# Scores two steps further ahead, later reciprocals and an even projection pace in a four-layer attention and Fourier kernel

## The chip, the cores and the metric

The program runs on one core of one Trainium2 chip. The metric is the time of one execution on the device in microseconds (us). A core has engines that run side by side, each with its own queue of instructions: TensorE (PE in the profile; its weight loads are listed as PEld), VectorE (DVE), ScalarE (ACT), GpSimd (POOL), and SyncE (SP), whose queue issues nearly all DMA transfers of this kernel. An instruction waits in its queue until the semaphores it names have been raised by other engines, and everything behind it waits with it. Matmuls write into eight banks of an accumulator memory (the tile `banks` in the profile), from which ScalarE or VectorE copy results away.

## The reference

Four layers on x of 2048 rows and 640 columns: attention, Fourier mixing, attention, Fourier mixing, each on the layernorm of x and added back. The change lies in attention, which has 32 heads of width 20, each row looking at itself and the 255 rows before it.

```python
qkv = (x @ wqkv).reshape(B, S, 3, H, Dh)          # q, k, v of (H, S, Dh)
scores = jnp.einsum("bhqd,bhkd->bhqk", q, k) * (Dh ** -0.5)
mask = (idx[:, None] - idx[None, :] >= 0) & (idx[:, None] - idx[None, :] < W)   # W = 256
p = _softmax(jnp.where(mask[None, None], scores, -1e9))
o = jnp.einsum("bhqk,bhkd->bhqd", p, v)
return o.reshape(B, S, D) @ wo
# Fourier layer: Cr @ (x @ Dr) - Ci @ (x @ Di), with cosine and sine matrices
```

All matmuls of the projections are done in three products of split numbers (a high part and a rest), for precision.

## The kernel before

An attention layer is `before_heads`, `heads` (L606) and `after_heads`. Before the heads, layernormed x is transposed into four row blocks of 512 (tiles `big0` to `big3`), v is computed, and so are the first two of ten chunks of the query and key projection. A chunk is 128 columns of the joined weights (tile `wc`) for all four row blocks. The other eight chunks are computed inside `heads`.

`heads` handles 32 heads as 8 quads of 4 heads, and 2048 rows as 16 blocks of 128, so there are 128 pairs of quad and block. The loop at L777 runs over steps from -LEAD to 128. In each step three things at different places of the 128 pairs are issued:

- *scores and maxima* at s = step + LEAD: L631 multiplies queries by keys for the four heads (two pairs, z = 0 and z = 1), and L636 on VectorE adds the mask and takes each row's maximum. Every fourth step (s divisible by 4) L644 transposes the maxima of four blocks on TensorE, L647 copies them, and L649 sends them by DMA as extra rows into the query tile `qp`.
- *exponentials* at t = step: L659 multiplies the other way round (keys by queries, with the row of maxima), L669 takes the exponential on ScalarE, and L675 and L679 blank the corners on GpSimd.
- *values* at v = step - 1: L694 multiplies probabilities by values, L701 copies the result to the tile `ou`, and every fourth step `finish` (L705) posts the load of the row sums (`sm`, L711), the store of the results (`o_d`, L712), the reciprocals (L714, VectorE) and their store (`r_d`, L717). The three numbers in `at` (L710) are the ticks at which these go out; a step has two ticks.

Steps below 0 have scores only; they are called the lead here. The banks of scores, exponentials and values are handed out by a planner's clock (`borrow`), from banks 0 to 3 in the lead and 0 to 5 after.

The projection fills what room TensorE has. It is cut into units of two matmuls of 64 x 512 on two halves of the array (`lockstep`, L257). Two row blocks make a set of two banks: 15 units on one half of the rows of the weights, then 15 on the other. Between the halves the second half waits for a small VectorE copy, `seen` (L263). A chunk is two sets, 60 units; the eight chunks have 480. When a set is done its two banks are copied by ScalarE (L544), cast and subtracted on GpSimd (L552, L211), and stored to `qk_d` (L524). From there `pack` (L582) posts twelve DMAs for each quarter of a quad (L594, three a step over four steps), into `qp` and `kp` of the next quad. They are due eight steps ahead of the scores that need them (six for quad 7), by the list `due` (L726). `fill(nf)` (L752) issues about nf units, rounded so that a half is divided evenly, after z = 0 of every step, and after z = 1 too in the lead. In the lead FIRST = 7 gives 8 and 7 units a step, 15 in all, and afterwards RATE = 4 gives four, four, four and three.

A set takes its two banks from a role (L48). Role `m` has banks 6 and 7 only; role `f` has 6, 7, 4 and 5, so that in the lead two sets are open at once, their halves one after the other.

```python
ROLES = {
    "m": (6, 7), "f": (6, 7, 4, 5), "w": (6, 7, 2, 3),
```

When the projection is done, the same `fill` issues partial output rows (`partials`, nine units a step, L257 with 64 x 320 and an addition L978) from the finished quads. They need o and its reciprocals loaded again from DRAM (`load_o`, L859 and L865) and x (L952). These start at step 97 in this kernel.

Of the kernel before, what the change touches and what calls it, by code (L numbers as in the profile page):

```python
# [21 lines left out]
NQ = H // 4  # L22
# [4 lines left out]
SCALE = DH ** -0.5  # L27
EPS = 1e-5

LEAD = 10  # L30
AHEAD = 8
EARLY = 3
AHEAD_X = 4
AFTER = 4
RATE = 4
FIRST = 7
LATE = 9
BACK = 2
PACE = 0.65
# [25 lines left out]
class Net:  # L65
# [89 lines left out]
    def next(self, name):  # L155
        i = self.turn.get(name, 0)
        self.turn[name] = i + 1
        tiles = getattr(self, name)[:3]
        return tiles[i % len(tiles)]
# [407 lines left out]

    def project(self):
        for c in range(2, NCH):
            lead = self.lead  # L570
            for sbs in ((0, 1, 2, 3),) if lead else ((0, 1), (2, 3)):
                if sbs[0] == 0 and c > 2:
                    self.load_chunk(c + 1)
                if sbs[-1] == 3:
                    self.cut_chunk(c + 1)
                if c == NCH - 1:
                    self.prepare(sbs[0])
                yield from self.pieces(c, sbs, "f" if lead else "m")
        self.prepare(4)
# [26 lines left out]
    def heads(self, xsrc, xdst, hook):  # L606
# [7 lines left out]
        def defer(d, fn):  # L614
            later.setdefault(now[0] + d, []).append(fn)
# [3 lines left out]
        def load_v(n):  # L619
            if n < 4 * NQ:  # L620
                nc.sync.dma_start(self.vq[n % 3][:, :384].rearrange("p (t c) -> p t c", c=96),
                                  self.vd[n // 4][:, n % 4 * 4:n % 4 * 4 + 4, :])
# [82 lines left out]
        def finish(quad, bk):  # L705
            ou = ous.pop((quad, bk))
            sm = pool.tile([P, 16], F32, name="sm", tag="sm")
            rc = pool.tile([P, 16], F32, name="rc", tag="rc")
            cols = slice(bk * 512, (bk + 1) * 512)
            at = (2, 9, 11) if quad < NQ - 1 else (1, 5, 6)  # L710
            self.post(at[0], lambda: nc.sync.dma_start(sm, ou[0:P:32, :]))  # L711
            self.post(at[0], lambda: nc.sync.dma_start(  # L712
                self.od[4 * quad:4 * quad + 4, :, cols].rearrange("h r s -> (h r) s"), ou))
            self.post(at[1], lambda: nc.vector.reciprocal(out=rc, in_=sm))  # L714

            def store():
                nc.sync.dma_start(  # L717
                    self.rd[bk, 4 * quad:4 * quad + 4, :].rearrange("h (a b) -> (h a) b", b=16), rc)
                self.post(2 if quad < NQ - 1 else 0, lambda: self.stored.add((quad, bk)))
            self.post(at[2], store)  # L720

        per_piece = 3 * KC
        total = NCH * NSB * per_piece
        done = [2 * NSB * per_piece]
# [27 lines left out]
        def fill(n):  # L752

            k, size = 0, 1
            while k < size:
                r = more()
                if r == 0 and k == 0:
                    continue
                if r != 1:
                    return  # L760
                k += 1
                if k == 1:
                    left = self.left + 1
                    size = -(-left // max(1, round(left / n)))
            if self.left == 0:
                more()
                if self.lead:
                    relieve()
                elif self.heavy:
                    self.heavy.sort(key=lambda h: h[0] not in ROLES["m"])  # L770
                    self.relieve()
# [4 lines left out]
        self.ring6 = dict.fromkeys((0, 1, 2, 3), -99.0)  # L776
        for step in range(-LEAD, steps + 1):  # L777
            now[0] = self.step = step
            clock = step * STEP
            if step == -1:  # L780
                self.ring6.update({4: -99.0, 5: -99.0})
            if step + LEAD == steps + 1:
                for b in ROLES["w"]:
                    self.ring6.pop(b, None)
            self.wide, self.lead, self.tiled = step + LEAD > steps, step < -2, step < steps - 1
            for f in later.pop(step, []):
                f()
            s, t, v = step + LEAD, step, step - 1
            if due and s >= due[0][0]:
                while done[0] < due[0][1]:  # L790
                    fill(15)
                q, j = due.pop(0)[2:]
                for i, f in enumerate(self.pack(q, j)):
                    defer(i // 3, f)
                for f in later.pop(step, []):
                    f()
            if v >= 0 and v % 4 == 3:
                load_v(v // 4 + 2)
            if done[0] < total:
                nf = max([FIRST if t < -2 else RATE + (t < 0)]  # L800
                         + [(d - done[0]) / max(1, at - s) for at, d, _, _ in due])
            else:
                nf = LATE
            rows = ((s - 1) // 16, ((s - 1) % 16) // 4) if 4 <= s < steps + 4 and s % 4 == 0 else None
            for z in range(2):
                if 0 <= t < steps:
                    banks = self.borrow_pair(clock + AT_T[z], HELD_T)
                    t_pair(t // 16, t % 16, z, banks)
                if 0 <= s < steps:
                    for e, b in enumerate(self.borrow(clock + AT_S[z], *HELD_S)):  # L810
                        s_head(s // 16, s % 16, 2 * z + e, b)
                if z and (rows or 0 <= v < steps):
                    last, = self.borrow(clock + AT_PV, HELD_PV)
                m = m_rows(*rows, last) if z and rows else iter(())
                next(m, None)
                if 0 <= t < steps:
                    t_exp(t // 16, t % 16, z, banks)
                    t_mask(t // 16, t % 16, z)
                if self.heavy:
                    self.heavy.sort(key=lambda h: h[0] not in ROLES["m"])  # L820
                    self.relieve()
                if z:
                    if 0 <= v < steps:
                        pv(v // 16, v % 16, last)
                    for _ in m:
                        pass
                if z == 0 or t < -1 or t >= steps:
                    fill(nf)
                self.tick()
            if step >= steps:  # L830
                self.load_to(step - steps + 2)
            if step > 16 * (NQ - 1):
                self.poll_late(step - 16 * (NQ - 1))
# [5 lines left out]
    def load_o(self, o, sb, k, raw=None, rr=None):  # L839
# [46 lines left out]

        busy = self.step + LEAD < 16 * NQ
        n, lane, eng = (2, "pool", nc.gpsimd) if busy else (1, "dve", nc.vector)
# [977 lines left out]
```

## Time and profile before

| what | us |
|---|---|
| median of the runs (lowest, highest) | 2182.82 (2181.66, 2192.8) |
| the profiled execution, its own time | 2187.93 |
| its span from the first to the last instruction | 2186.2 |
| heads of the first attention layer, lead to the last value | 404.1 |
| heads of the second attention layer | 401.2 |
| lead steps -10 to -3, first and second layer | 31.20, 30.70 |
| steps 0 to 91, first and second layer | 252.1, 252.2 |
| steps 97 to 117, first and second layer | 73.4, 72.9 |

The stages were cut where the first instruction of a step starts on TensorE: the first L631 for steps of the lead, the first L659 from step 0 on. A window's row has its length and then, for each engine, the microseconds in which it was busy and in brackets the number of its instructions; PE and PEld are the matmuls and the weight loads of TensorE. A row of the timeline has the start, the time taken by the whole group, the engine, the line of the kernel, and how many alike instructions were joined (x8); in brackets stands how long the engine was idle ahead of it and who ended that. A row of the kind "L544 ACT ACTIVATE x64: 578/599/609" gives minimum, median and maximum in nanoseconds. A row of waits names the engine and line that waited, who ended it, the sum, how often, and the longest. The granted clock is 1.00 nearly all through; it was half for 6.8 us in the first layer's heads (422.3 us) and for 3.4 us each at 599.8 and 1685.2.

### The profile page before, as it was taken

The page shows a single profiled execution, that of the slowest core. Times are in us where ns is not written, and L with a number is a line of the kernel's source. Part 1 is how long each engine was busy: PE and PEld are TensorE (multiplying, and loading weights), DVE is VectorE, ACT ScalarE, POOL GpSimd, SP SyncE. Part 2 cuts the span into 40 slices and gives each one's busy share as a digit, 9 for nine tenths or more (in the row PEclk, how much of TensorE's full clock was granted, in tenths as well). Part 3 has the DMA queues.
Part 4 walks back from the last instruction along what each step waited for, and adds up shares of the span by engine and source line. Part 5 has one row for each costly group of instructions (what it writes and reads, how often), then busy time and mean ns, then how long its engine had stood idle before and what let it go on. Part 6 is the DMA issues. An engine that isn't in the chain of part 4 may idle for free.

```text
span 2186.2 us, 48927 instructions
## 1 busy us (share of the span) xinstructions
PE 2118.1 (97%) x17872; PEld 1783.2 (82%) x17872; DVE 1603.7 (73%) x3931; ACT 1140.5 (52%) x2125; POOL 958.0 (44%) x1562
## 2 busy tenths in 40 slices
PE   7999999988999999999999999999899999999999
PEld 7987777677878888889999877776778888888899
DVE  6358888886897868786661588888767968677676
ACT  3117777656554545452341177777565645445332
POOL 3037776765614222322430377767655033231324
PEclk9999999999999999999999999999999999999999
DMA  5546666785555354656645556567855454546653
GB/s 183 175 157 190 198 180 215 211 224 169 202 192 189 127 183 141 214 177 207 207 156 167 162 186 200 181 212 226 216 161 182 140 182 132 174 152 208 222 165 125
DMA packets 227089, 398.40 MB, mean 182 GB/s; under 512 B 39969, under 2 KB 86561, under 8 KB 226849
## 3 DMA queue, kind: packets, MB, share of 16 engines
q1 hardware_dynamic: 226848, 395.28, 57.3%
q8 instruction: 141, 2.31, 0.5%
q14 instruction: 100, 0.81, 0.1%
HBM read 273.94 MB, written 120.06 MB: 180 GB/s over the span
## 4 chain that ended last, share of the span: by engine, by line
PE 78%; DVE 7%; DMA 5%; ACT 4%; issue 3%; POOL 2%; SPq 1%; ACTq 0%; DVEq 0%; POOLq 0%
PE banks L1416 29%; PE banks L239 15%; PE banks L257 12%; PE banks L694 6%; PE banks L659 5%; PE banks L1704 5%; PE banks L631 5%; DMA qp<-qk_d 2%; DVE banks L636 1%; ACT pt L669 1%; DMA x_d<-x 1%; PE banks L341 1%; DMA kp<-qk_d 1%; ACT big L1039 1%; DVE qp L232 1%
## 5 line engine op out<-in xcount | busy, mean ns | idle before, releaser
L636 DVE CUSTOM_DVE_ANT_0 banks<-banks,mask 128x384 f32<-128x384 f32 (+2 forms) x1024 | 527.6, 557 | 123.0 <-PE banks L631 99.9
L669 ACT ACTIVATE pt<-banks 128x768 f32<-128x768 f32 (+2 forms) x512 | 393.8, 772 | 168.7 <-PE banks L659 55.2
L675 POOL TENSOR_SCALAR_AFFINE_SELECT pt<-pt 128x256 f32<-128x256 f32 x512 | 213.3, 417 | 213.8 <-ACT pt L669 192.0
L257 PE MATMUL banks<-big,wc 64*128 64x512 f32 x1920 | 271.1, 394 | 0.4 <-DVE pt L442 0.4
L659 PE MATMUL banks<-qp,kp 61*128 61x384 f32 (+2 forms) x1024 | 210.2, 381 | 22.8 <-DVE mc L636 17.4
L694 PE MATMUL banks<-pt,vq 128*32 128x128 f32 x5760 | 211.6, 278 | 3.5 <-ACT pt L669 3.4
L631 PE MATMUL banks<-kp,qp 60*128 60x384 f32 (+2 forms) x1024 | 205.5, 347 | 6.7 <-DVE mc L636 3.1
L257 PEld LDWEIGHTS banks<-big,wc 64*128 64x128 f32 x1920 | 186.8, 185 | 22.6 <-ACT x L544 1.5
L679 POOL TENSOR_SCALAR_AFFINE_SELECT pt<-pt 128x256 f32<-128x256 f32 x448 | 193.8, 433 | 0.0
L226 ACT ACTIVATE qp<-pt 128x512 fp32r<-128x512 f32 (+1 forms) x200 | 123.2, 625 | 128.1 <-DVE pt L1347 51.7
L232 DVE TENSOR_TENSOR qp<-pt,qp 128x512 fp32r<-128x512 f32 (+1 forms) x198 | 156.6, 798 | 42.1 <-ACT qp L226 40.5
L694 PEld LDWEIGHTS banks<-pt,vq 128*32 128x32 f32 x5760 | 142.4, 110 | 51.5 <-issue 35.3
L659 PEld LDWEIGHTS banks<-qp,kp 61*128 61x128 f32 x1024 | 108.0, 184 | 87.3 <-DVE mc L636 65.2
L1416 PE MATMUL banks<-qp,big 128*128 128x512 f32 x648 | 152.9, 390 | 0.0
L631 PEld LDWEIGHTS banks<-kp,qp 60*128 60x128 f32 x1024 | 123.6, 186 | 31.9 <-DVE mc L636 16.4
L1345 POOL TENSOR_TENSOR pt<-pt,pt 128x512 f32<-128x512 f32 x32 | 47.2, 1475 | 231.4 <-DMA pt<-c 173.4
L226 ACT ACTIVATE c<-pt 128x512 fp32r<-128x512 f32 x146 | 90.4, 625 | 111.1 <-POOL pt L1325 57.1
L636 DVE DVE_READ_ACCUMULATOR2_ANT mc<- 128x1 f32 x1024 | 145.0, 142 | 0.0
L1416 PEld LDWEIGHTS banks<-qp,big 128*128 128x128 f32 x648 | 120.8, 188 | 24.2
L232 DVE TENSOR_TENSOR c<-pt,c 128x512 fp32r<-128x512 f32 x144 | 113.8, 793 | 26.9 <-ACT c L226 24.4
L1416 PE MATMUL banks<-qp,xc 128*128 128x512 f32 x480 | 117.4, 391 | 4.3 <-DVE xc L232 2.8
L552 POOL CAST c<-x 128x512 fp32r<-128x512 f32 x64 | 38.9, 611 | 166.5 <-ACT x L544 162.3
(253 smaller groups left out, 4479.9 us busy)
## 6 DMA issues: line engine op xcount, KB each, us to landing
pt<-c SPq DMA_DIRECT2D x166, 512.0 KB
qk_d<-c SPq DMA_DIRECT2D x80, 512.0 KB
kp<-qk_d SPq DMA_DIRECT2D x384, 80.0 KB
qp<-qk_d SPq DMA_DIRECT2D x384, 80.0 KB
kp<-u_d SPq DMA_DIRECT2D x32, 640.0 KB
o_d<-ou SPq DMA_DIRECT2D x64, 256.0 KB
x_d<-x SPq DMA_DIRECT2D x48, 320.0 KB
v_d<-pt SPq DMA_DIRECT2D x16, 768.0 KB
```

The source lines that it names most:

```text
L226: nc.scalar.activation(hi, src, AF.Copy, scale=-1.0 if neg else 1.0)
L232: (eng or nc.vector).tensor_tensor(out=lo, in0=src, in1=hi.bitcast(F32), op=OP.subtract)
L239: self.nc.tensor.matmul(p, x, y, start=n == 0, stop=n == last)
L257: self.nc.tensor.matmul(ps[a], x[r], y[r], start=half + i == 0, stop=half == 1 and i == n - 1, skip_group_check=True)
L631: nc.tensor.matmul(p, qp[quad % 2][b:b + 60, z, qb * P:(qb + 1) * P], kp[quad % 2][b:b + 60, z, k0 * P:(qb + 1) * P], start=True, stop=True)
L636: nc.vector.tensor_tensor_reduce(out=p, in0=p, in1=self.mask[:, 384 - n * P:], scale=1.0, scalar=NEG, op0=OP.add, op1=OP.max, accum_out=mc ...
L659: nc.tensor.matmul(self.banks[:, banks[e], :n * P], kp[quad % 2][b:b + 61, z, kb * P:(kb + 1) * P], qp[quad % 2][b:b + 61, z, kb * P:(kb + ...
L669: nc.scalar.activation(pt[quad, kb][:, 2 * z:2 * z + 2, :n * P], self.banks[:, b0:b1 + 1, :n * P], AF.Exp, scale=SCALE)
L675: nc.gpsimd.affine_select(out=t[:, :, 0:P], in_=t[:, :, 0:P], pattern=[[0, 2], [1, P]], compare_op=OP.is_ge, fill=0.0, base=0, channel_mul ...
L679: nc.gpsimd.affine_select(out=t[:, :, 256:384], in_=t[:, :, 256:384], pattern=[[0, 2], [-1, P]], compare_op=OP.is_gt, fill=0.0, base=0, ch ...
L694: nc.tensor.matmul(self.banks[32 * h:32 * h + 32, bank, :P], vq[:, 96 * (kb % 4) + 21 * h:96 * (kb % 4) + 21 * h + 32], t[:, h, (qb - kb) ...
L1416: nc.tensor.matmul(self.banks[:, bk, :], p, b[q], start=start and m == 0, stop=stop and last and m == 2, skip_group_check=True)
```

## The change

Five edits, all in `heads` and what it calls:

- LEAD is 12 instead of 10: scores and maxima run two steps further ahead, there are two more lead steps, and scores end at step 115 instead of 117.
- In the lead only chunk 2 is computed on four banks; chunk 3 and later use two banks, set after set.
- The pace after the lead is not 4 a step but the units left over the steps left until step 96. In the lead FIRST = 6 still gives 8 and 7.
- The list `due` is kept, and so is LATE.
- The reciprocals and their store go out at ticks 12 and 14 instead of 9 and 11, except for the first quarter of quad 5, which keeps the old ticks, and for quad 7, which keeps its own.

```diff
-LEAD = 10
+LEAD = 12
...
-RATE = 4
-FIRST = 7
+ROWS_AT = 96
+FIRST = 6
...
     def project(self):
         for c in range(2, NCH):
-            lead = self.lead
+            lead = self.lead and c == 2
             for sbs in ((0, 1, 2, 3),) if lead else ((0, 1), (2, 3)):
...
-            at = (2, 9, 11) if quad < NQ - 1 else (1, 5, 6)
+            at = (1, 5, 6) if quad == NQ - 1 else (2, 9, 11) if (quad, bk) == (NQ - 3, 0) else (2, 12, 14)
...
             if done[0] < total:
-                nf = max([FIRST if t < -2 else RATE + (t < 0)]
+                nf = max([FIRST if t < -2 else (total - done[0]) / max(1, ROWS_AT - t)]
                          + [(d - done[0]) / max(1, at - s) for at, d, _, _ in due])
```

The units of an attention layer come out like this in the built programs:

| steps | before | after |
|---|---|---|
| full lead steps | 8 steps, 15 units each | 10 steps, 15 units each |
| steps -2 and -1 | 10 and 5 | 8 and 4 |
| steps 0 to 91 | 345 | 306 |
| steps 92 to 95 | 0 | 12 |
| steps of three units, four units (0 to 95) | 23, 69 | 66, 30 |
| of these with a transpose of maxima | 0, 23 | 16, 8 |

*TensorE, lead, chunk 3, the end of the first half of its first set* (`big0` and `big1` are row blocks 0 and 1, `big2` and `big3` blocks 2 and 3; `wc_1190` holds the chunk's weights; in brackets the engine that is waited for). Before:

```order
L257 MATMUL banks_74<-big0_158,wc_1190 128x512
L257 MATMUL banks_74<-big1_341,wc_1190 128x512
L631 MATMUL banks_74<-kp0_561,qp0_106 128x384 [waits DVE_49] x2
L257 MATMUL banks_74<-big2_512,wc_1190 128x512 [waits Activation_49]
L257 MATMUL banks_74<-big3_732,wc_1190 128x512 [waits Activation_49]
L257 MATMUL banks_74<-big2_512,wc_1190 128x512
```

After:

```order
L257 MATMUL banks_74<-big0_158,wc_1190 128x512
L257 MATMUL banks_74<-big1_341,wc_1190 128x512
L631 MATMUL banks_74<-kp0_561,qp0_106 128x384 [waits DVE_49] x2
L257 MATMUL banks_74<-big0_158,wc_1190 128x512 [waits DVE_49]
L257 MATMUL banks_74<-big1_341,wc_1190 128x512
```

Before, the first half of the second set follows on two other banks, whose copies belong to a set that ended more than a step earlier. After, the second half of the same set follows, and it waits for the copy `seen` between the halves.

*TensorE, the end of that first set, half a step later.* After:

```order
L257 MATMUL banks_74<-big0_158,wc_1190 128x512
L257 MATMUL banks_74<-big1_341,wc_1190 128x512
L631 MATMUL banks_74<-kp0_561,qp0_106 128x384 [waits DVE_49] x2
L257 MATMUL banks_74<-big2_512,wc_1190 128x512 [waits Activation_49]
L257 MATMUL banks_74<-big3_732,wc_1190 128x512 [waits Activation_49]
```

The second set now starts on the same two banks, so its first unit waits for the ScalarE copies of the set that ended just ahead of the two L631.

*SP's queue, first layer, the first loads of quad 7* (`kp1` and `qp1` from `qk_d`) and the first o loads of the output rows (L859, L865). Before:

```order
L594 DMA kp1_104<-qk_d_82 20x2x512 x3
L952 DMA big2_5880<-x 128x640
L859 DMA x_6074<-o_d_85 128x1x512
L865 DMA rr2_103<-r_d_86 128x1x512
L859 DMA x_6077<-o_d_85 128x1x512
L711 DMA sm_6057<-ou1_100 128x1x16
L712 DMA o_d_85<-ou1_100 128x512
L717 DMA r_d_86<-rc_5906 128x16
L594 DMA qp1_105<-qk_d_82 20x2x512 x3
L859 DMA x_6147<-o_d_85 128x1x512
L865 DMA rr0_101<-r_d_86 128x1x512
```

After:

```order
L594 DMA kp1_104<-qk_d_82 20x2x512 x6
L717 DMA r_d_86<-rc_5712 128x16
L594 DMA qp1_105<-qk_d_82 20x2x512 x3
L621 DMA vq1_93<-v_d_83 128x384
L952 DMA big2_6044<-x 128x640 x2
L649 DMA qp0_106<-mt_6056 2x4x128 x2
L594 DMA qp1_105<-qk_d_82 20x2x512 x3
L952 DMA big2_6044<-x 128x640
L859 DMA x_6094<-o_d_85 128x1x512
```

Before, the o loads and the store of a quad's results stand between the loads of keys and queries; after, all twelve loads of the quarter come first.

## The prediction

> **What bounds the kernel now.** I read the page first, then a table of windows over the stages of one attention layer, then single steps, and last the rows of the instructions that the change moves.
>
> ```profile
> span 2186.2 us, 48927 instructions
> PE 2118.1 (97%) x17872; PEld 1783.2 (82%) x17872; DVE 1603.7 (73%) x3931; ACT 1140.5 (52%) x2125; POOL 958.0 (44%) x1562
> PE 78%; DVE 7%; DMA 5%; ACT 4%; issue 3%; POOL 2%; SPq 1%; ACTq 0%; DVEq 0%; POOLq 0%
> ```
>
> TensorE leads both the busy shares and the chain of waits, but these are means over stages. The windows cut the second attention layer's heads into the eight full lead steps, steps -2 and -1, steps 0 to 91, steps 92 to 96 (no projection left), steps 97 to 117, and the end without scores. Columns: length, then busy time and instructions per engine, granted clock, DMA share, GB/s.
>
> ```profile
> core 0: us, PE busy (x) PEld busy (x) DVE busy (x) ACT busy (x) POOL busy (x), PEclk, DMA share, GB/s
> 1216.90:1247.60 30.70, 30.70 (x276) 26.54 (x277) 19.65 (x73) 4.24 (x9) 11.30 (x17) 1.00 0.43 139
> 1247.60:1252.10 4.50, 4.50 (x41) 3.46 (x38) 3.37 (x12) 1.35 (x3) 3.41 (x6) 1.00 0.64 239
> 1252.10:1504.30 252.20, 247.73 (x3495) 187.72 (x3491) 210.05 (x787) 184.41 (x336) 184.44 (x422) 1.00 0.63 197
> 1504.30:1517.50 13.20, 11.58 (x165) 7.43 (x161) 11.83 (x43) 8.56 (x19) 11.21 (x24) 1.00 0.81 247
> 1517.50:1590.40 72.90, 65.23 (x1009) 53.96 (x1009) 59.56 (x201) 42.53 (x76) 44.88 (x99) 1.00 0.82 216
> 1590.40:1618.10 27.70, 25.07 (x399) 19.85 (x395) 12.29 (x23) 20.06 (x38) 20.35 (x43) 1.00 0.48 144
> ```
>
> The lead has TensorE busy all 30.70 us: there it is the bound. In steps 0 to 91 it shows 247.73 of 252.20, but its ends are modelled and its weight loads fill only 187.72, so single steps must say what a unit of projection (two matmuls) costs. Step 24 of that layer carries four units, from one first L659 to the next:
>
> ```profile
> 1318.20 0.44 PE L659 MATMUL banks<-qp,kp 61*128 61x384 f32 x2
> 1318.66 1.09 PE L257 MATMUL banks<-big,wc 64*128 64x512 f32 x8
> 1319.59 0.34 PE L659 MATMUL banks<-qp,kp 61*128 61x384 f32 x2
> 1320.85 0.44 PE L659 MATMUL banks<-qp,kp 61*128 61x384 f32 x2
> 1318.83 0.82 ACT L669 ACTIVATE pt<-banks 128x768 f32<-128x768 f32 x1 [0.21 <-PE banks L631]
> 1320.05 0.81 ACT L669 ACTIVATE pt<-banks 128x768 f32<-128x768 f32 x1 [0.41 <-DVE mc L636]
> ```
>
> It takes 2.65 us. The second exponential ends at 1320.86, where the next step's scores begin: beside TensorE there is a loop of scores, exponential and freed banks, about as long as the step. Whole steps show the price (rows: a new set's first units, three units, four units, four units with a transpose of maxima, and two with none):
>
> ```profile
> 1306.90:1309.80 2.90, 2.90 (x44) 2.12 (x40) 2.34 (x9) 2.64 (x6) 2.90 (x7) 1.00 0.44 143
> 1315.60:1318.20 2.60, 2.60 (x42) 1.93 (x38) 1.76 (x9) 2.05 (x4) 1.69 (x5) 1.00 0.76 273
> 1318.20:1320.90 2.70, 2.70 (x46) 2.15 (x42) 1.90 (x7) 1.91 (x3) 1.38 (x4) 1.00 0.60 175
> 1323.50:1326.40 2.90, 2.90 (x45) 2.35 (x41) 2.56 (x10) 1.91 (x4) 1.65 (x5) 1.00 0.62 183
> 1504.30:1506.90 2.60, 2.51 (x36) 1.60 (x32) 2.31 (x9) 2.12 (x5) 2.60 (x7) 1.00 0.64 211
> 1506.90:1509.50 2.60, 2.17 (x36) 1.46 (x33) 2.32 (x10) 1.79 (x3) 2.60 (x7) 1.00 0.62 184
> ```
>
> A step without any unit still takes 2.60, one with three takes 2.60, one with four 2.65: in the body a unit is mostly covered by the loop.
>
> **The change, per attention layer.** (1) *Two more lead steps.* Each full lead step is 30.70 / 8 = 3.84 us and holds 15 units, which stay at 15. Two more cost 7.7. The transposes of the maxima come on steps -8, -4 and 0 instead of -6 and -2, so the lead holds one more (0.28, below): **+8.0**. TensorE is wholly busy there, so nothing hides it.
>
> ```profile
> 1224.41 0.36 PE L631 MATMUL banks<-kp,qp 60*128 60x384 f32 x2
> 1224.58 2.01 PE L257 MATMUL banks<-big,wc 64*128 64x512 f32 x16
> 1226.41 0.36 PE L631 MATMUL banks<-kp,qp 60*128 60x384 f32 x2
> L257 PE MATMUL banks<-big,wc 64*128 64x512 f32 x290 | 42.4, 395 | 0.0
> L544 ACT ACTIVATE x<-banks x64: 578/599/609, 137.1 to 1504.2; 128x512 f32<-128x512 f32 x64
>   PEld banks L257: 1.5, 9
> L263 DVE COPY seen<-banks x60: 153/159/163, 129.6 to 1607.1; 128x2 f32<-128x2 f32 x60
> L644 PE MATMUL banks<-ident,mc x64: 277/277/278, 142.9 to 1592.3; 128*16 128x128 f32 x64
> ```
>
> The first three rows give a unit's price on a full TensorE: from 1224.58 to 1226.41 sixteen matmuls issue, 1.83 / 8 = 0.23 us a unit.
>
> (2) *Two banks in the lead.* Only chunk 2 now runs on four banks. From chunk 3 on, a new set's first unit waits for the two L544 copies of the set just ended, with one pair of L631 between. The last matmul's 0.39, then two copies of 0.60, less the pair's 0.36, leave 1.2 to 1.3 us of TensorE standing, at the starts of steps -6 and -4: +2.6. Likewise both halves of a set, with only that pair between, now wait for L263: 0.39 and 0.16, less the pair's 0.36, and a hand-over between engines, about 0.25 each, three times, +0.7. Sum **+3.3**. The same waits in the whole trace cost 1.5 us in nine, but in the body 1.3 us and more of other work stands between (1319.59 to 1320.85 above, and the next scores). Bounds: 0, if copies start earlier than the order says, and 5, with three full copy waits and the L631 pair hiding nothing. Behind the waiting L257 stand the next L631, so the maxima slip too; nobody waits for these yet.
> The Trainium skill, "Perfetto Trace Analysis", section "Matmuls", says that independent matmul groups should rotate through different banks, so that the evacuation of one overlaps the next group's matmuls; this speaks against the edit, and by it the +3.3 would be the result, where the nine waits of this trace alone, 0.17 each, would make it +0.5.
>
> (3) *Steps -2 and -1* hold 12 units instead of 15 (-0.7) but, by the order, a third copy wait at -2 (+1.1): **+0.4**.
>
> (4) *Steps 0 to 95.* 345 units before, 318 after, and the last 12 of these in steps 92 to 95, which had none. Of 24 transposing steps 16 have three units where all had four but one: (2.90 - 2.60) less the transpose's own share, 0.2 each, -3.2. Of the plain steps 27 more have three units: 2.65 - 2.59, so -1.5. One set fewer is started, -0.3 (2.90 against 2.65). Units in 92 to 95 hide behind POOL, which is busy 2.60 of 2.60 there, 0.05 each: +0.2. Sum **-4.8**. Bounds: 0, since a step with no unit is no shorter, and -9.0, 39 units less in steps 0 to 91 at 0.23. I take the middle, since the rows of steps lie near the low end and only the dear steps promise more.
> Of rule and row: the Trainium skill, "Perfetto Trace Analysis", section "Identifying the Most-Contended Engine", holds matmul busy time to be no good measure of how full TensorE is, and weight-load busy a better one; here that is 74% (187.72 of 252.20) against 98%. By it the price stays near the step rows; by the 98% it would be -9.0.
>
> (5) *First loads of quad 7.*
>
> ```profile
> PE banks L631 <- DMA qp<-qk_d: 2.0, 1, 2.0
> PE banks L631 <- DMA kp<-qk_d: 1.0, 1, 1.0
> PE banks L659 <- DMA qp<-mt: 1.1, 1, 1.1
> 412.90:427.80 14.90, 13.27 (x167) 8.52 (x163) 12.40 (x45) 8.70 (x19) 12.11 (x26) 0.81 0.67 213
> 1525.77 2.27 SPq L594 DMA_DIRECT2D qp<-qk_d  x3
> 1531.11 1.26 SPq L594 DMA_DIRECT2D qp<-qk_d  x3
> ```
>
> The scores of quad 7 waited 2.0 us in the second layer and 1.0 in the first, since their loads stand on SP's queue behind o loads, a reciprocal's store and the vq load. In the new order all twelve come ahead of the first o loads: **-1.5**. Bounds: -2.0, and +1.5 if now the o loads come late for the first output rows, which wait behind them. The first layer's 1.1 on a row of maxima lies in a stretch of clock 0.81; taken as gone, -1.1 once.
>
> (6) *Scores end two steps earlier.*
>
> ```profile
> 1584.00:1587.40 3.40, 3.10 (x56) 2.57 (x52) 2.98 (x10) 2.54 (x5) 1.85 (x5) 1.00 0.65 184
> 1587.40:1590.40 3.00, 3.00 (x52) 2.54 (x52) 2.79 (x12) 1.97 (x3) 2.88 (x6) 1.00 0.49 133
> 1599.50:1602.40 2.90, 2.74 (x46) 2.25 (x46) 0.75 (x2) 1.93 (x4) 2.63 (x6) 1.00 0.74 242
> L714 DVE RECIPROCAL rc<-sm x64: 240/248/254, 186.3 to 1624.0; 128x16 f32<-128x16 f32 x64
> ```
>
> Steps 116 and 117 take 3.40 and 3.0, a like step without scores 2.9: **-0.6**. *Reciprocals* move by half a step or more on VectorE, which has 42 us free in steps 0 to 91 (0.46 a step): 0. If that cover is gone, because one now stands ahead of a maximum that frees a bank, each costs its 0.25, at most 28 of them, +7. Their r_d stores move behind on SP's queue, and the first output rows, at step 97, need none of the later ones.
>
> Sum: 8.0 + 3.3 + 0.4 - 4.8 - 1.5 - 0.6 = +4.8 a layer, two layers +9.6, less 1.1: **+8.5 us**. The profiled execution took 2187.93 us, 1.7 of it outside the span; it would become 2196.4. It stood 5.1 above the median of the runs, so against the median the forecast is 2182.82 + 8.5 = **2191.3**.
>
> **The rivals.** *R1, the body gains at full price.* TensorE is the bound throughout, so moved units are free and those taken away from the body pay 0.23, while the copies hide. Per layer 8.0 - 0.7 - 9.0 - 1.5 - 0.6 = -3.8, in all -8.7: 2174. For it: 98% busy, transposing steps of 2.90 with weight loads of 2.35. Against: step 23 with two matmuls fewer is 0.06 shorter, not 0.23. If instead all 96 steps reached 2.59 (252.2 and four empty steps, 10.4, against 248.6: -14.0) the sum comes to the same, with (2) at its price.
>
> *R2, the copies are hidden.* (2) is 0 and (3) -0.7: per layer +0.4, in all -0.3: 2182.5. For it: nine copy waits cost 1.5 us. Against: just two L631 between.
>
> *R3, slower: the loop sets every body step.* If score, exponential, bank and POOL leave no step below what it has, (4) is 0, and if the loads in (5) keep their place in time, since L594 also waits for the pieces' stores, that is 0 too: per layer 8.0 + 3.3 + 0.4 - 0.6 = +11.1, in all 2205. It decides if three-unit transposing steps still take 2.8 or more. For it: the 2.60 us of empty steps; against: the 2.90 of the four-unit ones.
>
> *R4, the stores behind the later reciprocals hold up output rows.* A block of rows waits 1.5 steps, 3.9 us, once a layer: 8.5 + 7.8, 2199. Against: the one block that opens the output rows keeps its old ticks.
>
> **How the numbers follow.** Forecast 0.38, R1 0.24, R2 0.16, R3 0.16, R4 0.06. Half a per cent, 10.9 us, is about what a measurement of this kernel tells from no change. Faster (below 2171.9): somewhat over half of R1's own spread of 2165 to 2182, with a little of R2, 0.16. Slower (above 2193.7): R3, R4 and two fifths of the forecast's own spread of 2184 to 2199, 0.38. Same: 0.46. Range 2171 to 2206: R1's better third and R3's worse half, hardly 0.2 together, lie outside.
>
> **What would show it.** Ten lead steps of 3.84 with TensorE standing over 1 us, L257 waiting for L544, at steps -6, -4, -2; a body of 96 steps near 258 us where it was 262.6; transposing steps near 2.7; no wait of L631 for quad 7's loads. Wrong if lead steps stay wholly busy (R2), if the body falls below 254 (R1) or stays above 261 (R3), or if L257 of the output rows waits for loads (R4).

## The result, and the profile after

| | us |
|---|---|
| kernel before, median of 5 runs | 2188.61 |
| changed kernel, median of 5 runs (lowest, highest) | 2203.74 (2201.75, 2208.12) |
| ratio, after to before, with its 95% interval | 1.0078 [1.0062, 1.0094] |
| span of the profiled execution, before and after | 2186.2, 2199.8 |
| heads of the first layer, before and after | 404.1, 415.3 |
| heads of the second layer, before and after | 401.2, 410.4 |

The change makes the kernel slower by 0.8%, 15 us by the medians and 17 by the ratio; 8.5 was forecast. The forecast added its 8.5 to a median of three runs of the kernel before, 2182.82; with five runs it is 2188.61. The page of the changed kernel has TensorE a point higher on the chain of waits:

```profile
span 2199.8 us, 48960 instructions
PE 79%; DVE 7%; DMA 5%; ACT 3%; issue 2%; POOL 2%; SPq 1%; ACTq 0%; DVEq 0%; POOLq 0%
```

The windows over the stages of the second layer's heads, cut like those of the kernel before: ten full lead steps, steps -2 and -1, 0 to 91, 92 to 96, 97 to 117, and the end.

```profile
core 0: us, PE busy (x) PEld busy (x) DVE busy (x) ACT busy (x) POOL busy (x), PEclk, DMA share, GB/s
1222.30:1264.70 42.40, 40.85 (x343) 32.96 (x344) 23.84 (x90) 5.59 (x12) 15.89 (x24) 1.00 0.44 149
1264.70:1270.00 5.30, 4.42 (x34) 3.03 (x30) 3.67 (x12) 1.80 (x4) 4.27 (x6) 1.00 0.65 210
1270.00:1518.10 248.10, 244.05 (x3411) 181.63 (x3411) 208.62 (x785) 182.07 (x328) 174.64 (x409) 1.00 0.62 190
1518.10:1532.50 14.40, 13.72 (x190) 9.41 (x186) 12.31 (x44) 10.47 (x22) 12.08 (x25) 1.00 0.71 206
1532.50:1604.80 72.30, 64.70 (x1001) 52.98 (x1001) 55.66 (x186) 42.75 (x78) 47.09 (x103) 1.00 0.79 226
1604.80:1632.70 27.90, 24.67 (x398) 19.82 (x402) 10.68 (x21) 19.81 (x36) 20.41 (x44) 1.00 0.49 147
```

Stage by stage against before: the lead +11.7, steps -2 and -1 +0.8, steps 0 to 91 -4.1, steps 92 to 96 +1.2, steps 97 to 117 -0.6, the end +0.2: 9.2 us, the whole of 410.4 less 401.2. The loss is the lead; steps 0 to 91 give a third of it back. In the lead TensorE is no longer busy throughout (40.85 of 42.40), and the timeline of TensorE shows why. The starts of step -6 (chunk 3's second set) and of step -4 (chunk 4's first), each with the units ahead of it:

```profile
1244.07 1.75 PE L257 MATMUL banks<-big,wc 64*128 64x512 f32 x14
1245.66 0.34 PE L631 MATMUL banks<-kp,qp 60*128 60x384 f32 x2
1246.64 2.37 PE L257 MATMUL banks<-big,wc 64*128 64x512 f32 x15 [0.65 <-ACT x L544]
1253.39 1.75 PE L257 MATMUL banks<-big,wc 64*128 64x512 f32 x14
1254.98 0.34 PE L631 MATMUL banks<-kp,qp 60*128 60x384 f32 x2
1255.96 0.99 PE L257 MATMUL banks<-big,wc 64*128 64x512 f32 x3 [0.65 <-ACT x L544]
```

Behind the last unit of a set comes one pair of L631, then TensorE stands 0.65 us until the first L544 copy frees its bank; weight loads of L257 wait for copies too, so step -6 as a whole is 1.18 us longer. From first L631 to first L631, steps -7 to -3 took 4.14, 4.97, 4.35, 5.59 (with a transpose) and 4.16 us where a full lead step of the kernel before took 3.79. Over the whole trace the rows of L544, and below them those of L714, say:

```profile
L544 ACT ACTIVATE x<-banks x64: 591/597/624, 133.9 to 1528.9; 128x512 f32<-128x512 f32 x64
  PEld banks L257: 9.1, 18
  PE banks L257: 3.9, 6
L714 DVE RECIPROCAL rc<-sm x64: 195/245/254, 199.3 to 1638.5; 128x16 f32<-128x16 f32 x64
who waited for it (us, times):
```

Waits for copies grew from 1.5 us (nine times) to 9.1 at the weight loads and 3.9 at the matmuls, six of these 0.65 each: three a layer, where the prediction put them, though each is shorter than the 1 us that it named. No engine waits for the reciprocals.

The wait for quad 7 did not go. Before, queries for its first block were late at step 102; now those for its second quarter (blocks 4 to 7) are, at step 104. First the second layer's, on TensorE's timeline; then the waits and the window of that step in the first layer:

```profile
1555.70 0.41 PE L631 MATMUL banks<-kp,qp 60*128 60x384 f32 x1
1557.63 0.41 PE L631 MATMUL banks<-kp,qp 60*128 60x384 f32 x1 [1.52 <-DMA qp<-qk_d]
```

```profile
PE banks L631 <- DMA qp<-qk_d: 1.7, 1, 1.7
PE banks L631 <- DMA qp<-mt: 1.3, 1, 1.3
455.60:464.70 9.10, 6.12 (x53) 4.66 (x53) 3.83 (x11) 2.22 (x4) 3.76 (x9) 0.62 0.72 199
```

The first layer stood 1.7 and 1.3 us there, with a granted clock of 0.62 over a step of 9.1 us.

Heads grew by 20.4 us in the two layers, the span only by 13.6. The rest of these two profiles differs by 6.8 the other way: the first heads start 3.2 us earlier, and in the Fourier layers the waits of L1704 for L1540 are 2.3 us in three where they were 7.5 in six. Each view has its heading and one row of it, first of the kernel before and then of the changed kernel:

```profile
its engine sat idle before it (us, times) until:
  DVE pt L1540: 7.5, 6
```

```profile
its engine sat idle before it (us, times) until:
  DVE pt L1540: 2.3, 3
```

In the profiles of the experiments this wait lies between 2.4 and 6.3 us without following any one edit, so I count it to no part of the change; how much of it belongs to single executions stays open.

### The profile page after: what moved, and what is told of

Its sections match the earlier page's. It is cut to its first block, busy times and chain, and to the rows that moved or that the text cites. A ratio compares the mean times of both kernels' runs of the same rounds, so it can differ in the third digit from the quotient of the medians.

```text
span 2199.8 us, 48960 instructions
## 1 busy us (share of the span) xinstructions
PE 2132.3 (97%) x17872; PEld 1783.3 (81%) x17872; DVE 1593.9 (72%) x3931; ACT 1143.2 (52%) x2125; POOL 954.0 (43%) x1562
## 4 chain that ended last, share of the span: by engine, by line
PE 79%; DVE 7%; DMA 5%; ACT 3%; issue 2%; POOL 2%; SPq 1%; ACTq 0%; DVEq 0%; POOLq 0%
PE banks L1416 30%; PE banks L239 15%; PE banks L257 11%; PE banks L694 6%; PE banks L1704 6%; PE banks L659 5%; PE banks L631 5%; DVE banks L636 2%; DMA qp<-qk_d 2%; ACT pt L669 1%; DMA qk_d<-c 1%; PE banks L341 1%; ACT big L1039 1%; POOL rs L1087 1%; DVE qp L232 1%
## 5 line engine op out<-in xcount | busy, mean ns | idle before, releaser
L257 PE MATMUL banks<-big,wc 64*128 64x512 f32 x1920 | 278.1, 396 | 4.8 <-ACT x L544 3.9
L659 PE MATMUL banks<-qp,kp 61*128 61x384 f32 (+2 forms) x1024 | 207.9, 379 | 21.3 <-DVE mc L636 16.6
L631 PE MATMUL banks<-kp,qp 60*128 60x384 f32 (+2 forms) x1024 | 219.4, 358 | 6.3 <-DMA qp<-qk_d 3.4
L257 PEld LDWEIGHTS banks<-big,wc 64*128 64x128 f32 x1920 | 188.0, 185 | 30.9 <-ACT x L544 9.1
L659 PEld LDWEIGHTS banks<-qp,kp 61*128 61x128 f32 x1024 | 106.3, 184 | 86.3 <-DVE mc L636 62.4
L631 PEld LDWEIGHTS banks<-kp,qp 60*128 60x128 f32 x1024 | 126.5, 185 | 42.7 <-DVE mc L636 23.9
```

What stands on the lines that cost most here:

```text
L257: self.nc.tensor.matmul(ps[a], x[r], y[r], start=half + i == 0, stop=half == 1 and i == n - 1, skip_group_check=True)
L631: nc.tensor.matmul(p, qp[quad % 2][b:b + 60, z, qb * P:(qb + 1) * P], kp[quad % 2][b:b + 60, z, k0 * P:(qb + 1) * P], start=True, stop=True)
L659: nc.tensor.matmul(self.banks[:, banks[e], :n * P], kp[quad % 2][b:b + 61, z, kb * P:(kb + 1) * P], qp[quad % 2][b:b + 61, z, kb * P:(kb + ...
```

## The experiments

Three theories were set against each other. A: the lead pays, two steps and the bank waits. B: lead waits are made up for later. C: pace, reciprocals and SP's queue take the time. The kernel before was timed beside all eleven runs; its medians there were 2189.03 to 2189.39. To give the ratios in us I multiply by 2189.

**Four banks for chunk 3.**

```diff
-            lead = self.lead and c == 2
+            lead = self.lead and c <= 3
```

> The changed kernel, but chunk 3 too is computed on four banks in the lead. Theory A (the lead pays: two steps of 3.79 us each and 3.8 us of bank and half-boundary waits a layer): the waits at the starts of steps -7, -6 and -5 go (0.35 + 1.2 + 0.55) and part of that at -4, so 2 to 3 us a layer, 4 to 6 in all: 9 to 11 us above the kernel before instead of 15. Rival B (the waits in the lead are made up for in the body, where the copies then come later): no change, 15 above. Rival C (the time goes in the body and in SP's queue, not in the lead): no change either, with the lead shorter in the trace and the body longer.

Measured: 2200.61, ratio 1.0054 [1.004, 1.0068], 12 us above before. The window over its ten lead steps:

```profile
1221.50:1260.50 39.00, 38.92 (x345) 31.54 (x344) 24.41 (x90) 5.60 (x12) 16.47 (x24) 1.00 0.48 157
```

39.0 where the changed kernel took 42.4: 3.4 us a layer, and TensorE is busy again. The body stayed the same (steps 1 to 91: 244.7 and 245.2 against 244.8 and 244.6). The lead is as A has it, and B falls for the body. In the times the gain is 5 us (A had 4 to 6, and 9 to 11 above the kernel before), though the two intervals just overlap. Not all of its 7 by the lead is kept: in the second layer step 104 took 7.91 us here, against 6.04.

**Ten lead steps**, with the banks of before; pace and reciprocals of the change stay.

```diff
-LEAD = 12
+LEAD = 10
-            lead = self.lead and c == 2
+            lead = self.lead
```

> The changed kernel with ten lead steps and its banks as before: only the even pace and the later reciprocals are left of the change. Theory A: all of the 11.8 us a layer in the lead go and some 3 us of body come back: within 4 us of the kernel before, so 12 to 18 us below the changed kernel. Rival C (the pace and the reciprocals cost the time): 8 us or more above the kernel before.

Measured: 2183.89, ratio 0.9979 [0.9968, 0.999], 5 us below the kernel before. The whole loss of the change is in LEAD and the banks that go with it: 22 us against the changed kernel, more than A's 12 to 18. Against the run ahead it is 16 us, 8.2 a layer, which is the net of two lead steps (39.0 less 30.6, 8.4 in the traces) and of all that shifts with them. C falls. But the scores' wait got worse here; TensorE and the granted clock at step 102 of the second layer:

```profile
1526.96 0.45 PE L659 MATMUL banks<-qp,kp 61*128 61x384 f32 x2 [0.76 <-DMA qp<-mt]
1530.47 0.44 PE L631 MATMUL banks<-kp,qp 60*128 60x128 f32 x1 [2.98 <-DMA qp<-qk_d]
1530.48 2.94 PE L257 MATMUL banks<-big,big 64*128 64x320 f32 x18
```

```profile
1526.00:1528.00 2.00, 0.74 (x11) 0.40 (x3) 0.94 (x6) 1.46 (x4) 1.50 (x4) 1.00 0.92 251
1528.00:1530.50 2.50, 0.03 (x2) 0.06 (x2) 0.00 (x0) 0.32 (x1) 1.46 (x3) 0.58 0.88 216
1530.50:1533.90 3.40, 3.40 (x24) 3.14 (x24) 0.80 (x3) 0.13 (x1) 0.00 (x0) 0.50 0.77 187
```

Here TensorE stands 3 us and then works at half its clock for 3.4 us more: eighteen matmuls take 2.94, where such eighteen took 1.48 to 1.49 at the full clock.

**Old ticks of the reciprocals**, on the changed kernel.

```diff
-            at = (1, 5, 6) if quad == NQ - 1 else (2, 9, 11) if (quad, bk) == (NQ - 3, 0) else (2, 12, 14)
+            at = (2, 9, 11) if quad < NQ - 1 else (1, 5, 6)
```

> The changed kernel with the old ticks of the reciprocals and their stores. Theory A: hidden, within 3 us of the changed kernel (12 to 18 us above the kernel before). Rival C: if a reciprocal between the two halves of a step holds up a maximum, 0.25 us at up to 28 places a layer come back, 5 to 14 us less than the changed kernel.

Measured: 2211.18, ratio 1.0098 [1.0082, 1.0113], 21 us above: slower than the changed kernel if anything, which neither theory had. Steps 1 to 91 are the same to 0.2 us, so a reciprocal costs nothing there at this pace. What differs is step 104 of the second layer: 9.45 us against 6.04, with a wait of 3.2 us for `qp` from `qk_d` and a stretch of half clock. The intervals overlap by 0.1%. With ten lead steps the same edit changes nothing: the run ahead has the later ticks and 2183.89, the run with the even pace alone, below, the old ones and 2183.8. So the ticks matter at most together with the wait at step 104; whether they do stays open.

**Old pace**, on the changed kernel.

```diff
-                nf = max([FIRST if t < -2 else (total - done[0]) / max(1, ROWS_AT - t)]
+                nf = max([FIRST if t < -2 else 4 + (t < 0)]
```

> The changed kernel with the old pace of four, four, four and three units a step after the lead, so that the projection ends about ten steps before the output rows. Theory A (a unit in the body costs about 0.05 us in a plain step and 0.2 in a step that transposes maxima): the same number of units in fewer steps, 1 to 3 us a layer more, 17 to 21 us above the kernel before. Rival R1 (each unit costs its 0.23 us wherever it stands): no change, 15 above.

Measured: 2204.43, ratio 1.007 [1.0053, 1.0086], 15 us above, as R1 said, but not for R1's reason (the profiled execution took 2212.1). Steps 0 to 91 took 252.1 and 251.5 us in the two layers, 3.7 and 3.4 more than the changed kernel, with 315 units. To price the thirty units that the longer lead takes out of the body, the next run is the one to compare with, since it has this pace and these reciprocals and ten lead steps: 345 units in 253.4 us in both layers. They are worth 1.3 and 1.9 us, 0.04 to 0.06 each and not R1's 0.23. Steps 97 to 117 took 71.9 and 70.9, 2.9 and 1.3 less than the changed kernel: with the projection done earlier, quad 7's scores did not wait at step 104 (4.45 us against 6.04). Part of this was lost at step 96 (5.2 and 5.1 against 3.3).

**Later reciprocals alone**, on the kernel before.

```diff
-            at = (2, 9, 11) if quad < NQ - 1 else (1, 5, 6)
+            at = (1, 5, 6) if quad == NQ - 1 else (2, 9, 11) if (quad, bk) == (NQ - 3, 0) else (2, 12, 14)
```

> The kernel before with only the later reciprocals of the change. The changed kernel with the old ticks was 22 us above the kernel before instead of 15, while its steps 1 to 91 took the same. Theory Q (later reciprocals help, by what follows them on SP's queue): 3 to 7 us below the kernel before. Theory A as first held (hidden): within 2 us of it.

Measured: 2189.36, ratio 1.0003 [0.999, 1.0015]. Hidden in the times; Q falls. In the trace steps 0 to 91 took 253.4 us in both layers, 1.3 more than before, 0.06 in each step with a transpose of maxima (2.93 against 2.87): a cost that the interval can't tell from nothing, and that the even pace does not show (248.7 and 248.6 with later ticks, 248.6 and 249.0 with the old ones).

**Even pace alone**, on the kernel before.

```diff
-                nf = max([FIRST if t < -2 else RATE + (t < 0)]
+                nf = max([FIRST if t < -2 else (total - done[0]) / max(1, ROWS_AT - t)]
```

> The kernel before with only the even pace of the change. Theory A (a unit in a short step costs less than one in a step that is already long): steps 1 to 91 shorter by 3.4 us a layer, as in the run with ten lead steps, against 2 to 4 us a layer more of waiting for the loads of quad 7, since the last chunk is stored later: within 3 us of the kernel before. Theory P (the pace is what helps): 4 us or more below.

Measured: 2183.8, ratio 0.9975 [0.9961, 0.9989], 5.5 us below: P's number. Its windows over steps 0 to 91 and 92 to 96 of the second layer:

```profile
1246.10:1495.20 249.10, 245.87 (x3477) 187.04 (x3473) 210.88 (x787) 182.53 (x332) 181.25 (x418) 1.00 0.66 197
1495.20:1509.20 14.00, 13.58 (x189) 9.35 (x185) 12.24 (x44) 10.18 (x21) 11.82 (x24) 1.00 0.69 187
```

249.1 and 14.0 against 252.2 and 13.2 before, with 336 units in steps 0 to 91 instead of 345, and 12 instead of none after; 0.7 us more is gained in steps -2 and -1. The changed kernel has 30 units less there than the run with ten lead steps, which shares its pace and its reciprocals, and is only 0.3 and 0.5 us shorter (248.4 and 248.1 against 248.7 and 248.6). So what helps the body is the pace, not the smaller number of units; what in the pace, the last run shows. A's 3.4 is right in size (3.5 and 3.1), and it had a price at the end: steps 97 to 117 took 76.1 and 78.0, 2.6 and 5.2 more than before, where it said 2 to 4. Its time, within 3 us, was missed. In this profile heads gain just 0.2 us in sum, and the other 4.7 of the span lie outside them, L1704's waits among them (2.7 us against 7.5). That the pace helps is measured; that the 5.5 us come from the body is not.

**Quad 7's loads two steps earlier**, on the changed kernel, and the same on the run with ten lead steps.

```diff
-        due = [(16 * q + 4 * j - AHEAD + 2 * (q == NQ - 1),
+        due = [(16 * q + 4 * j - AHEAD,
```

> The changed kernel with the loads of quad 7 due two steps earlier, like those of the other quads. Theory A (the wait of the scores for queries of quad 7, 1.5 to 3 us at step 104, was only moved there by the change): that wait goes, 2 to 4 us a layer, 4 to 8 us less than the changed kernel, 7 to 11 above the kernel before. Rival (the loads then hold up the output rows' own loads behind them): no change, 15 above, with waits of L257 on loads at steps 97 to 101.

> Ten lead steps, banks as before, even pace, later reciprocals, and quad 7's loads two steps earlier. The run without the last was 5 us below the kernel before, with scores waiting 3.7 us at step 102 of the second layer's heads. Theory A: without this wait 3 to 5 us a layer less, 11 to 15 us below the kernel before. Rival: output rows wait instead, 5 us below.

Measured: 2204.1, ratio 1.0078 [1.0056, 1.01], and 2185.06, ratio 0.998 [0.9967, 0.9993]: no change in either. On the changed kernel the wait at step 104 is gone (4.37 us in the second layer against 6.04), but steps 98 and 99 grew from 3.55 and 3.03 to 5.12 and 4.55. The waits of the changed kernel with earlier loads, between 1535 and 1542 us:

```profile
PE banks L659 <- DVE mc L636: 2.6, 2, 2.2
DVE big L978 <- DMA big<-x_d: 1.8, 1, 1.8
```

The addition of the first output row waits 1.8 us on VectorE for its load of x, the maxima stand behind it in VectorE's queue, and TensorE waits 2.2 us for them. With ten lead steps the second layer's step 102 fell from 8.46 to 3.47 us, and step 101 grew from 3.85 to 5.97, since the L659 behind it now waits 2.9 us for a row of maxima. The rival is right in substance, at other lines than it named: in both runs the loads that went first made others late.

**Eight and nine lead steps**, with the old reciprocals, even pace, chunk 3 on two banks.

```diff
-LEAD = 12
+LEAD = 8
```

> Even pace alone, as in the run that was 5.5 us below the kernel before, but eight lead steps, chunk 3 on two banks. Theory A, taken the other way: two lead steps of 3.8 us less a layer, 30 units more in the body at 0.05 to 0.2 us (1.5 to 6), about 1 us of half-boundary and bank waits more: 0 to 5 us a layer less, so 6 to 14 us below the kernel before. Rival (a lead of eight is too short: the row of maxima goes out two steps ahead of its first reader, with two DMA of it on SP's queue): L659 waits for the rows of maxima, 1 us or more at each quarter of a quad, 32 a layer: 40 us or more above.

> The same with nine lead steps and chunk 3 on two banks. Theory A: one lead step of 3.8 us less a layer, 15 units more in the body (1 to 3), 2 us of bank waits more: within 2 us a layer of the run with ten, so 2 to 8 us below the kernel before. Rival (too short, as with eight): L659 waits for rows of maxima, 10 us or more above.

Measured: eight, 2255.55, ratio 1.0305 [1.0279, 1.0331], 67 us above; nine, 2194.17, ratio 1.0024 [1.0011, 1.0037], 5 us above. The waits for rows of maxima, first of the run with eight (all waits) and then of the run with nine (those of L659):

```profile
PE banks L659 <- DMA qp<-mt: 68.1, 31, 6.1
```

```profile
  DMA qp<-mt: 14.3, 5
```

With eight the rows of maxima come 2.2 us late in the mean, 31 times: 68.1 us, as much as the whole loss, although the lead is 7.2 us a layer shorter than with ten; the trace also has twelve stretches of half clock from the first heads on. The rival holds. With nine neither theory had the time. Two of its five waits, at the change to the output rows, make up 12.2 of the 14.3 us; steps 0 to 91 took 254.2 and 254.1 us, 5 more than with ten, with only 1.0 us of such waits in each, and the two-bank waits of chunk 3 are 1.5 us a layer of its lead (steps of 4.14 and 4.97). So a shorter lead did not pay as tried here; nine steps with four banks for chunk 3 were not tried.

**Even pace to step 93**, ten lead steps, old reciprocals.

```diff
-ROWS_AT = 96
+ROWS_AT = 93
```

> Even pace alone with ten lead steps, but the projection spread to step 93 instead of 96, so that the last pieces are stored three steps earlier. Theory A (the even pace gives 3.3 us a layer in the body and gives part of it back by the waits for quad 7's loads, which come with the last pieces): the body loses about 0.5 us a layer, the wait at step 102 falls from 4.2 us to 2 or less: 8 to 12 us below the kernel before. Rival (the loads stand behind the output rows' loads on SP's queue whatever the pieces do): unchanged waits, 4 to 6 us below.

Measured: 2181.66, ratio 0.9967 [0.9954, 0.998], 7 us below the kernel before, 1 short of A's 8 to 12; its interval and that of the pace to 96 overlap. In the second layer step 102 is at 4.66 us instead of 8.53, and steps 97 and 98 at 4.55 and 4.69 instead of 3.02 and 3.70, so that steps 97 to 117 gain 1.0 us of the 78.0. Steps 0 to 91 hold 345 units again, as in the kernel before, and take 250.9 and 249.4 us where that takes 252.1 and 252.2.

This run shows what in the pace helps, and it is not evenness. In steps 4 to 87 both kernels have 315 units, 21 steps of three and 63 of four, in the same round of four steps; this run takes 226.6 and 226.9 us there, the kernel before 229.9 in both layers. Only the place differs. Before, the three-unit step is the last of a round that starts at a step divisible by 4, and half a set or a whole one ends in it; now it is the first of that round, so sets end and are copied one step later. Steps 27 and 28 of the second layer, first of the kernel before (three units, then four), then of this run (four, then three):

```profile
1326.41:1329.01 2.60, 2.60 (x43) 1.91 (x39) 2.06 (x9) 2.45 (x6) 1.79 (x5) 1.00 0.06 15
1329.01:1331.88 2.87, 2.87 (x44) 2.11 (x41) 2.32 (x9) 2.23 (x5) 2.87 (x7) 1.00 0.57 173
```

```profile
1321.57:1324.20 2.63, 2.63 (x44) 2.04 (x40) 1.95 (x9) 2.00 (x4) 1.41 (x4) 1.00 0.30 86
1324.20:1326.80 2.60, 2.60 (x42) 1.91 (x38) 2.38 (x9) 2.35 (x6) 1.91 (x5) 1.00 0.40 128
```

In the mean of steps 4 to 87 of this layer, the first step of a round took 2.77 us with four units and 2.62 with three, the last one 2.55 with three and 2.58 with four. A unit is worth 0.15 in the one and 0.04 in the other. The pace to step 96 with ten lead steps has most of its three-unit steps (20 of 29) in the first place as well. Whether the units themselves or the ends of sets, which moved with them, are cheaper there stays open.

This has the lowest time of all versions tried, below both kernels; it is the kernel before with the pace rule of the change, ending three steps earlier.

## Why the prediction came out as it did

The direction and the range held (2203.74 in 2171 to 2206). The size did not: +8.5 against 15 to 17, and the likeliest outcome, within half a per cent, was missed (0.78%). That it came no further out is in part luck: by the profiles the heads, the only place that the sum has, lost 20.4 us, and 6.8 came back outside them, of which the sum says nothing. By the steps of the sum, for the second layer:

| step of the prediction | forecast | measured | from |
|---|---|---|---|
| (1) two lead steps and a transpose | +8.0 | +8.0 | 2 x 3.79, and 0.43 more in a lead step with a transpose |
| (2) two banks in the lead | +3.3 | +3.8, 3.4 of it undone by four banks for chunk 3 | steps -7 to -3; first run |
| (3) steps -2 and -1 | +0.4 | +0.8 | windows |
| (4) steps 0 to 95, with 96 | -4.8 | -2.9 | windows |
| (5) wait for quad 7 | -1.5 | 0 (about +2 in the first layer) | steps 97 to 117 less (6) |
| (6) scores end earlier | -0.6 | -0.6 | steps 116 and 117: 6.43, now 5.81 |
| reciprocals | 0 | 0 | 1.0003 alone; +1.3 in that trace's steps 0 to 91 |
| end without scores | not in the sum | +0.2 | windows |
| a layer | +4.8 | +9.2 | |

**Right.** The lead was priced by its own rows, where TensorE is full, and came out to 0.1 us. The wait on two banks was read from the order and the copy's time; rival R2, that the copies hide, is refuted by the first run. Of the 3.8 the starts of sets took 2.55 (2.6 was forecast) and the three half boundaries 1.3 (0.7 was), so the 0.25 put for each was too low. By the Trainium skill's rule on rotating banks ("Perfetto Trace Analysis", section "Matmuls") the +3.3 was to be the result, and the trace agrees with 3.4 to 3.8. A unit in the body is worth little: between runs that differ by the lead alone, with its banks, thirty fewer took 0.3 and 0.5 us off steps 0 to 91 at the even pace and 1.3 and 1.9 at the old one, where R1 had 0.23 us for each, 6.9 in all.

**Mis-sized, and for a wrong reason.** Step (4) was 1.9 us too hopeful, and its terms came out otherwise than they were put. Its largest term was "(2.90 - 2.60) less the transpose's own share, 0.2 each, -3.2" for sixteen transposing steps with three units. Cut at the first L659, the 21 transposing steps among steps 4 to 87 of the second layer took 60.4 us before and 60.4 after: nothing was gained. Their means are 2.87 us with four units before, and 3.03 with four (7 steps) and 2.80 with three (14) after. Within the changed kernel the unit is worth its 0.2; but the two further lead steps moved the transposes from the third step of a round of four to the first, where such a step is dearer with the same four units, so against before only 0.07 was gained. The run with the old pace has 3.03 there as well, so this comes with the lead. The 63 plain steps took 169.5 us before and 164.7 after, -4.8, where -1.5 was put: 42 of them have three units (2.56) and 21 four (2.72), where 21 had three (2.55) and 42 four (2.76). The price of a plain unit, 0.06, was read from two neighbouring steps; by place it is 0.04 to 0.15, as the run to step 93 shows. The ends of the body then took back what this gained: steps 88 to 91 lost 0.7 us and steps 92 to 96 1.2, not 0.2.

**Wrong.** Step (5) failed: "In the new order all twelve come ahead of the first o loads" is so (but for one that stands ahead of quad 7's loads in both kernels), and nothing came of it. The loads of quad 7 follow the scores, which run two steps further ahead; the o loads follow the end of the projection, which does not come earlier. So it is now the second quarter's loads that fall among the o loads, the loads of x and the stores of the last pieces: on SP's queue they go out from 1539.23 to 1554.83 us, and step 104's scores get them at 1557.63. I looked at the first quarter alone and took a moved wait for a removed one. In the first layer it was dearer still, with half clock at step 104 (9.01 us against 6.04): two layers of heads lost 20.4 us, not 9.6. The term of -1.1, counted once, fell with it. And I made nothing of what lies outside the heads, where the two profiles differ by 6.8 us the other way.

R3's time (2205) is nearest to the measured 2203.74, but only because both stand on different medians of the kernel before: as a difference it is +22.2 against +15.1, about as far off as the forecast's +8.5. Its sign for transposing steps came true (2.80, "2.8 or more"), and the loads in (5) keep their wait; its sign for the body did not, for 96 steps took 259.2 us, near the forecast's 258 and not above 261. R4's +16.3 is nearest as a difference, and that is luck: in the changed kernel no L257 of the output rows waits for a load, and later reciprocals alone leave the time as it is. Something there does hold up loads, but by the two runs with earlier loads it is the order of the transfers.

## What to carry to other kernels

Price a longer run-ahead by the stage where the bounding engine is already full: each step added there is paid in full, while the work it takes from the steady loop comes back at that loop's own price, here 0.3 to 1.9 us a layer for thirty units; which of the loop's steps got the smaller share mattered more than how much work there was. Where a queue of transfers is what is short, as SP's at the change from projection to output rows, moving a load earlier moves the wait to the next load in line; look at every load behind it before taking a wait off the sum. Try the parts of a bundled change singly: one part here, the pace, was worth 5 us and was hidden under 22 us lost by another. Compare runs that differ in one thing: beside the kernel before, whose reciprocals differ too, the thirty units would seem worth nothing at the old pace.

## What the runs showed of the hardware

After a long stand of TensorE the granted clock was half for 3.4 us or twice that. In the twelve profiles other than that with eight lead steps there are 15 stands of 2.15 us and longer behind the start of the first heads, and at 14 of them the clock is 0.5 during the stand or within the next microseconds; the one without was of 2.87 us. Of nine stands between 1.9 and 2.1 us, one had it. The wait of 2.05 us at step 102 of the kernel before kept its full clock, that of 2.98 us with ten lead steps did not (0.58, then 0.50 in the rows shown). So a wait can cost more than its length: there eighteen matmuls took twice their time after it. But a long stand is not the only way: the same twelve profiles have 44 stretches of half clock from the first heads to shortly before the end, and 30 of them have no such stand at them. All three of the kernel before are of this kind; the longest stands close ahead of them are 0.43, 1.05 and 1.05 us. So no length of a stand is shown to be the limit, and that a stand is the cause was not tried by itself.
